# Linear attention and a leaky-ReLU feed-forward on one core: chunk order, transpose path and scheduler changed

## The chip, the cores and the metric

One core of a Trainium2 chip runs the whole kernel. The metric is the device time in microseconds of one execution; three runs of the kernel before gave 204.39 us as their median (204.13 to 206.44).

## What is computed

A recurrent attention with a decaying state runs over 4 batches, 8 heads, 768 positions and a head size of 48; its output, as 3072 tokens of 384 numbers, goes through a feed-forward of width 2048.

```python
for t in range(S):
    cur = einsum('bhd,bhe->bhde', u * k[t], v[t])
    y[t] = einsum('bhd,bhde->bhe', r[t], state + cur)
    state = w[t][..., None] * state + einsum('bhd,bhe->bhde', k[t], v[t])
x = y.transpose(0, 2, 1, 3).reshape(B * S, H * D)
h = x @ w_in                      # 384 -> 2048
out = maximum(0.01 * h, h) @ w_out  # 2048 -> 384
```

Inputs and output are float32; matmuls run in bfloat16.

## The kernel before

The positions are cut into chunks of 128, so there are 24 chunks, six for each batch. For each chunk the attention makes these steps, one instruction or one short group of instructions each:

- SP's DMA queue loads w, k, r and v (L290, 192 KB each, in pieces of 192 B) into one of 11 `in` buffers.
- ACT takes the logarithm of w (L310, `lw`); TensorE sums it from the chunk's far end with the triangular matrix `trev` (L325) and, where there is a state, gives its totals per head (L330). DVE adds `lw` to that sum (L340, `ci`); ACT takes the two exponents `er` (L347) and `ek` (L353), and DVE multiplies r and k by them (L360, L366) into the two halves of `rk`.
- TensorE transposes `rk` in eight pieces (L379) into the PSUM tile `sc`; DVE and ACT copy the halves out (L387, L389) as `rkT`. TensorE makes the scores from `rkT` (L450), into `sc` again, and DVE masks them into `m` (L471).
- GpSimd prepares the diagonal part (L406, L410, with DVE's L414, then L418 into `vs`), casts v (L316) and decays the state (L439, `sb`). TensorE's sums (L461) and DVE's addition (L485) make the next state.
- TensorE multiplies state and masked scores by their operands (L497, L501) into `yp`, DVE adds `vs` and makes `y` (L512). TensorE transposes `y` in three pieces (L521), and ACT copies it into the chunk's columns of `xT` (L527).

The feed-forward takes a block of chunks, here always one. Its up part is four groups of 12 matmuls of 128 columns (L553) into one of two `hp` tiles, each emptied by ACT with the leaky ReLU into `g` (L587). Its down part is four groups of 4 matmuls of 384 columns (L605) into one of two `op` tiles, which DVE copies out (L616) and SP's queue stores (L620). The weights come in 8 DMAs of 768 KB (L243, L248) and are cast by DVE and ACT in halves (L266, L268).

Chunks run through batch 0, then batch 1, and so on, so that a chunk's state is that of the chunk just before it. The order of the instructions on each engine isn't the order of the program. The class `Plan` keeps each step's engine, duration, dependencies and priority, plays the engines against each other, and puts the steps out by the times at which they started in that play. Attention has priority `P0 = n * 10`, the feed-forward 1000 and more, ACT's leaky ReLU 5. The logarithm of chunk n must not be planned before the first up group of chunk n - LEAD, and its loads not before the cumulation of chunk n - AHEAD. `Ring` gives buffers out in turn, as the program is written. On the chip each engine, and SP's queue, takes its instructions strictly in that order.

Of the kernel before, what the change touches and what calls it, by code (L numbers as in the profile page):

```python
# [14 lines left out]

class Plan:
# [3 lines left out]
    LAT = {"PE": 0.28, "DVE": 0.07, "ACT": 0.07, "POOL": 0.07, "SP": 0.07}  # L20

    def __init__(self):
        self.eng, self.dur, self.fn, self.deps, self.pri, self.wire = [], [], [], [], [], []

    def add(self, eng, dur, fn, deps, pri, wire=None):

        i = len(self.eng)
        self.eng.append(eng)
        self.dur.append(dur)
        self.fn.append(fn)  # L30
        self.deps.append(sorted({d for d in deps if d is not None}))
        self.pri.append(pri)
        self.wire.append(wire)
        return i

    def order(self):
        n = len(self.eng)
        users = [[] for _ in range(n)]
        left = [len(d) for d in self.deps]
        for i, d in enumerate(self.deps):  # L40
            for j in d:
                users[j].append(i)
        ready_at = [0.0] * n
        start, done = [None] * n, [0.0] * n
        free = {e: 0.0 for e in self.ENGINES}
        coming = {e: [] for e in self.ENGINES}
        ready = {e: [] for e in self.ENGINES}
        dma_free = 0.0
        for i in range(n):
            if not left[i]:  # L50
                heapq.heappush(coming[self.eng[i]], (0.0, i))
        events = [(0.0, e) for e in self.ENGINES]
        heapq.heapify(events)
        count = 0
        while events:
            now, e = heapq.heappop(events)
            if free[e] > now + 1e-9:
                continue
            while coming[e] and coming[e][0][0] <= now + 1e-9:
                _, i = heapq.heappop(coming[e])  # L60
                heapq.heappush(ready[e], (self.pri[i], i))
            if not ready[e]:
                if coming[e]:
                    heapq.heappush(events, (coming[e][0][0], e))
                continue
            _, i = heapq.heappop(ready[e])
            start[i] = now
            count += 1
            free[e] = now + self.dur[i]
            if self.wire[i] is None:  # L70
                done[i] = free[e] + self.LAT[e]
            else:
                dma_free = max(dma_free, free[e]) + self.wire[i]
                done[i] = dma_free + 1.5
            heapq.heappush(events, (free[e], e))
            for j in users[i]:
                left[j] -= 1
                ready_at[j] = max(ready_at[j], done[i])
                if not left[j]:
                    f = self.eng[j]  # L80
                    heapq.heappush(coming[f], (ready_at[j], j))
                    heapq.heappush(events, (max(ready_at[j], free[f]), f))
        assert count == n, (count, n)
        self.start, self.done = start, done
        return sorted(range(n), key=lambda i: (start[i], i))


class Ring:


    def __init__(self, tiles):
        self.tiles = tiles
        self.steps = [[] for _ in tiles]
        self.n = -1

    def take(self):
        self.n += 1
        k = self.n % len(self.tiles)
        old, self.steps[k] = self.steps[k], []
        return Use(self.tiles[k], old, self.steps[k])  # L100


class View:


    def __init__(self, use, t):
        self.t, self.old, self.steps = t, use.old, use.steps


class Use:  # L110
    def __init__(self, t, old, steps):
        self.t, self.old, self.steps = t, old, steps
# [3 lines left out]
def kernel(  # L116
# [23 lines left out]
    NPE = 24  # L140
    LEAD = 4
    AHEAD = 5

    WEIGHTS = [(2, 14)] * 4 + [(4, 34)] * 4
    blocks = [1] * NCH
# [3 lines left out]
    psum = ctx.enter_context(tc.tile_pool(name="psum", bufs=1, space=bass.MemoryType.PSUM))  # L149

    def ring(name, count, shape, dtype, where=None):
        return Ring([(where or pool).tile(shape, dtype, name=f"{name}{i}") for i in range(count)])


    trev = pool.tile([128, 128], BF16, name="trev")
    maskb = pool.tile([128, 128], BF16, name="maskb")
# [6 lines left out]

    in_r = ring("in", 11, [128, 1536], F32)
    lw_r = ring("lw", 3, [128, H, 64], BF16)
    ci_r = ring("ci", 2, [128, H, D], F32)
    er_r = ring("er", 3, [128, H, D], F32)
    ek_r = ring("ek", 2, [128, H, D], F32)
    rk_r = ring("rk", 4, [128, 2, H, 64], BF16)
    rkT_r = ring("rkT", 4, [128, 2 * NP, 128], BF16)  # L170
    vb_r = ring("vb", 6, [128, H, D], BF16)
    ru_r = ring("ru", 2, [128, H, D], F32)
    dg_r = ring("dg", 3, [128, H], F32)
    vs_r = ring("vs", 4, [128, H, D], F32)
    m_r = ring("m", 3, [128, 2, NP, 128], BF16)
    a_r = ring("a", 3, [128, NP, 2], F32)
    sx_r = ring("s", 3, [128, NP, 2, D], F32)
    sb_r = ring("sb", 3, [128, NP, 2, D], BF16)
    y_r = ring("y", 4, [128, H, D], BF16)
    g_r = ring("g", 4, [128, NJ, max(blocks) * L], BF16)  # L180
    o_r = ring("o", 4, [128, DM], F32)

    hp_r = ring("hp", 2, [128, 512], F32, psum)
    op_r = ring("op", 2, [128, DM], F32, psum)
    cp_r = ring("cp", 1, [128, 512], F32, psum)
    yp_r = pp_r = ring("yp", 1, [128, 512], F32, psum)
    sc_r = ring("sc", 1, [128, 2, NP, 128], F32, psum)

    with tc.manual_schedule():
        nc.scalar.preload_act_table_set("natural_log_exp_and_others")  # L190
        for t in lw_r.tiles + rk_r.tiles:
            nc.vector.memset(t[:], 0.0)
        for t in a_r.tiles:
            nc.gpsimd.memset(t[:], 0.0)
        nc.vector.memset(ones[:], 1.0)
        nc.vector.memset(trev[:], -1.0)

        nc.gpsimd.affine_select(
            out=trev[:], in_=trev[:], compare_op=ALU.is_ge, fill=0.0,
            base=0, pattern=[[-1, 128]], channel_multiplier=1,  # L200
# [7 lines left out]

# [7 lines left out]
        def step(eng, dur, fn, pri, reads=(), writes=(), deps=(), wire=None):  # L216

            d = list(deps)
            for x in writes:
                d += x.old  # L220
            i = plan.add(eng, dur, fn, d, pri, wire)
            for x in (*reads, *writes):
                x.steps.append(i)
            return i

        def dve(n, src=60):
            return (src + n) / 960.0 + 0.05

        def act(n, src=180):
            return (src + n) / 1200.0 + 0.02  # L230

# [4 lines left out]
        JQ = NJ // NQ  # L236

        def weight_steps(q, which, pri):
            st = in_r.take()

            def load(st=st, q=q):
# [11 lines left out]
            ld = step("SP", 0.45, load, pri, writes=[st], wire=2.2)  # L253
            made = []
            for half, eng in ((0, "DVE"), (1, "ACT")):
                def cast(st=st, q=q, half=half, eng=eng):
# [8 lines left out]
                    if eng == "DVE":  # L265
                        nc.vector.tensor_copy(out=o, in_=i)  # L266
                    else:
                        nc.scalar.copy(out=o, in_=i)  # L268
                d = 0.65 if eng == "DVE" else act(768, 224)
                made.append(step(eng, d, cast, pri, reads=[st], deps=[ld]))  # L270
            (win_s if which == 0 else wout_s).append(made)


        xt_steps, cums, lns = [], [], []
        prev = None
        for n in range(NCH):
            b, c = divmod(n, C)
            t0 = c * L
            P0 = n * 10
            for i, (before, pri) in enumerate(WEIGHTS):  # L280
                if n == before:
                    weight_steps(i % NQ, i // NQ, pri)
            first, last = c == 0, c == C - 1
            slot = in_r.take()
            wn, kn, rn, vn = (
                View(slot, slot.t[:, i * DM : (i + 1) * DM].rearrange("p (h d) -> p h d", h=H)) for i in range(4))
            lds = []
            for src, use in ((w, wn), (k, kn), (r, rn), (v, vn)):
                def load(src=src, use=use, b=b, t0=t0):
                    nc.sync.dma_start(  # L290
                        out=use.t, in_=src[b, :, t0 : t0 + L, :].rearrange("h p d -> p h d")
                    )
                lds.append(step(
                    "SP", 0.45, load, P0, writes=[slot], wire=0.97,
                    deps=[cums[n - AHEAD]] if n >= AHEAD else []))
            if n == 0:
                u_ld = step(
                    "SP", 0.5,
                    lambda: nc.sync.dma_start(
                        out=ub[:], in_=u.rearrange("h d -> (h d)").partition_broadcast(128)  # L300
                    ),
                    P0, wire=0.6,
# [3 lines left out]
            lw = lw_r.take()  # L306
# [234 lines left out]
        for nb, size in enumerate(blocks):  # L541
# [17 lines left out]
            for ch in chs:  # L559
                for q in range(4):  # L560
                    m2.append((ch, q, g, (ch - chs[0]) * L))
# [97 lines left out]
```

## Time and profile before

| what | value |
|---|---|
| median of three runs | 204.39 us |
| the profiled execution's span | 203.9 us |
| its first matmul starts at | 4.49 us |
| its last stretch of down matmuls | 196.75 to 200.02 us |
| TensorE busy | 179.8 us (88%) |
| DVE, ACT, GpSimd busy | 140.6, 120.7, 102.4 us |
| DMA | 30.46 MB, mean 149 GB/s |

The profile is of one execution. "Busy" counts a matmul from its start to its modelled end, and matmuls overlap in the pipeline, so a busy TensorE is not one at its peak. A row of the groups names line, engine and operation, the tiles written and read, shapes and count, then busy us and mean ns, and then the idle time before these instructions with what ended it. The slices cut the span into 40 equal parts of 5.1 us; a digit is the busy share in tenths.

### The profile page before, as it was taken

The page shows a single profiled execution, that of the slowest core. Times are in us where ns is not written, and L with a number is a line of the kernel's source. Part 1 is how long each engine was busy: PE and PEld are TensorE (multiplying, and loading weights), DVE is VectorE, ACT ScalarE, POOL GpSimd, SP SyncE. Part 2 cuts the span into 40 slices and gives each one's busy share as a digit, 9 for nine tenths or more (in the row PEclk, how much of TensorE's full clock was granted, in tenths as well). Part 3 has the DMA queues.
Part 4 walks back from the last instruction along what each step waited for, and adds up shares of the span by engine and source line. Part 5 has one row for each costly group of instructions (what it writes and reads, how often), then busy time and mean ns, then how long its engine had stood idle before and what let it go on. Part 6 is the DMA issues. An engine that isn't in the chain of part 4 may idle for free.

```text
span 203.9 us, 6000 instructions
## 1 busy us (share of the span) xinstructions
PE 179.8 (88%) x2448; PEld 141.5 (69%) x2448; DVE 140.6 (69%) x231; ACT 120.7 (59%) x265; POOL 102.4 (50%) x126
## 2 busy tenths in 40 slices
PE   0436866999999999699997999999999999999992
PEld 0326754677878878477785777878887787788770
DVE  6588379758889994999769987876885585431111
ACT  3334985667875568267674675766865756644430
POOL 2581094248879995988869967365321110100000
PEclk9999995799999999999999999999999999999999
DMA  6999999999999999999979874691101101110002
GB/s 126 201 292 364 171 230 378 249 196 177 201 184 218 181 191 222 196 189 199 217 155 240 163 166 107 119 189 46 39 2 43 39 3 42 39 39 23 27 33 77
DMA packets 107178, 30.46 MB, mean 149 GB/s; under 512 B 100368, under 2 KB 105616, under 8 KB 107152
## 3 DMA queue, kind: packets, MB, share of 16 engines
q1 hardware_dynamic: 107152, 30.09, 69.4%
q8 instruction: 19, 0.31, 0.7%
q14 instruction: 7, 0.06, 0.1%
HBM read 25.36 MB, written 4.72 MB: 148 GB/s over the span
## 4 chain that ended last, share of the span: by engine, by line
PE 68%; DVE 11%; ACT 6%; DMA 5%; POOL 3%; issue 2%; SPq 1%; DVEq 0%
PE op L605 26%; PE hp L553 25%; PE sc L379 5%; PE sc L450 3%; DVE rk L366 2%; DMA in<-in_r_dram 2%; DMA in<-in_w_dram 2%; PE yp L501 2%; DVE m L471 2%; PE cp L325 2%; DVE rkT L387 2%; DVE rk L360 2%; ACT g L587 2%; PE yp L461 1%; PE yp L521 1%
## 5 line engine op out<-in xcount | busy, mean ns | idle before, releaser
L587 ACT ACTIVATE g<-hp 128x512 bf16<-128x512 f32 x96 | 57.3, 599 | 48.1 <-PE hp L553 47.5
L553 PE MATMUL hp<-xT,w_in_b 128*128 128x128 bf16 x1152 | 80.4, 220 | 1.3 <-ACT xT L527 0.9
L605 PE MATMUL op<-w_out_b,g 128*128 128x384 bf16 x384 | 78.2, 330 | 0.0
L553 PEld LDWEIGHTS <-w_in_b 128*128 128x128 bf16 x1152 | 70.5, 99 | 9.0 <-issue 1.0
L605 PEld LDWEIGHTS <-g 128*128 128x128 bf16 x384 | 33.3, 98 | 14.2 <-issue 0.7
L471 DVE TENSOR_TENSOR m<-sc,maskb 128x1024 bf16<-128x1024 f32 x24 | 29.3, 1220 | 11.4 <-PE sc L450 9.9
L406 POOL TENSOR_TENSOR ru<-in,ub 128x384 f32<-128x384 f32 x24 | 24.9, 1037 | 16.5 <-DMA in<-in_r_dram 15.7
L439 POOL TENSOR_TENSOR sb<-s,a 128x384 bf16<-128x384 f32 x20 | 18.5, 924 | 25.3 <-ACT a L432 23.4
L418 POOL TENSOR_TENSOR vs<-in,dg 128x384 f32<-128x384 f32 x24 | 22.3, 931 | 17.1 <-DVE y L512 12.1
L616 DVE COPY o<-op 128x384 f32<-128x384 f32 x24 | 13.3, 552 | 19.3 <-PE op L605 19.2
L410 POOL TENSOR_TENSOR ru<-ru,in 128x384 f32<-128x384 f32 x24 | 25.7, 1071 | 0.4
L379 PE MATMUL sc<-ident,rk 128*128 128x128 bf16 x192 | 19.2, 230 | 5.6 <-DVE rk L360 3.2
L389 ACT COPY rkT<-sc 128x512 bf16<-128x512 bf16 x24 | 14.1, 586 | 14.5 <-PE sc L379 7.1
L366 DVE TENSOR_TENSOR rk<-in,ek 128x384 bf16<-128x384 f32 x24 | 21.8, 907 | 0.0
L360 DVE TENSOR_TENSOR rk<-in,er 128x384 bf16<-128x384 f32 x24 | 18.3, 765 | 3.4 <-ACT er L347 2.3
L379 PEld LDWEIGHTS <-rk 128*128 128x128 bf16 x192 | 13.4, 101 | 10.3 <-DVE rk L360 4.3
L316 POOL CAST vb<-in 128x384 bf16<-128x384 f32 x24 | 12.9, 536 | 10.5 <-DMA in<-in_v_dram 8.6
L414 DVE TENSOR_REDUCE dg<-ru 128x8 f32<-128x384 f32 x24 | 13.1, 545 | 6.4 <-POOL ru L410 6.3
L512 DVE TENSOR_TENSOR y<-yp,vs 128x384 bf16<-128x384 f32 x24 | 13.2, 552 | 5.3 <-PE yp L501 4.5
L340 DVE TENSOR_TENSOR ci<-cp,lw 128x384 f32<-128x384 f32 x24 | 13.2, 548 | 3.8 <-PE cp L330 2.9
L347 ACT ACTIVATE er<-cp 128x384 f32<-128x384 f32 x24 | 11.9, 495 | 6.2 <-DVE ci L340 6.1
L310 ACT ACTIVATE lw<-in 128x384 bf16<-128x384 f32 x24 | 12.6, 523 | 2.5 <-DMA in<-in_w_dram 2.4
(39 smaller groups left out, 160.8 us busy)
## 6 DMA issues: line engine op xcount, KB each, us to landing
in<-in_w_dram SPq DMA_DIRECT2D x24, 192.0 KB, 4.4
in<-in_k_dram SPq DMA_DIRECT2D x24, 192.0 KB, 4.6
in<-in_r_dram SPq DMA_DIRECT2D x24, 192.0 KB, 4.6
in<-in_v_dram SPq DMA_DIRECT2D x24, 192.0 KB, 4.3
out_dram<-o SPq DMA_DIRECT2D x24, 192.0 KB, 3.2
in<-in_moe_w_in_dram SPq DMA_DIRECT2D x4, 768.0 KB, 8.3
in<-in_moe_w_out_dram SPq DMA_DIRECT2D x4, 768.0 KB, 7.7
ub<-in_u_dram SPq DMA_DIRECT2D x1, 192.0 KB, 4.4
```

What stands on the lines that cost most here:

```text
L360: lambda rk=rk, rn=rn, er=er: nc.vector.tensor_tensor(out=rk.t[:, 0, :, 0:D], in0=rn.t, in1=er.t[:], op=ALU.mult),
L366: lambda rk=rk, kn=kn, ek=ek: nc.vector.tensor_tensor(out=rk.t[:, 1, :, 0:D], in0=kn.t, in1=ek.t[:], op=ALU.mult),
L379: nc.tensor.transpose(trv[:, a, g, :], rk.t[:, a, 2 * g : 2 * g + 2, :].rearrange("p h d -> p (h d)"), ident[:])
L389: nc.scalar.copy(out=o, in_=i)
L406: lambda ru=ru, rn=rn: nc.gpsimd.tensor_tensor(out=ru.t[:], in0=rn.t, in1=ubv, op=ALU.mult),
L410: lambda ru=ru, kn=kn: nc.gpsimd.tensor_tensor(out=ru.t[:], in0=ru.t[:], in1=kn.t, op=ALU.mult),
L418: lambda vs=vs, vn=vn, dg=dg: nc.gpsimd.tensor_tensor(out=vs.t[:], in0=vn.t, in1=dg.t[:].unsqueeze(2).to_broadcast([128, H, D]), op=ALU.mult),
L439: lambda sb=sb, s_in=s_in, a_in=a_in: nc.gpsimd.tensor_tensor(out=sb.t[:].rearrange("p g a d -> p (g a) d"), in0=s_in.t[:].rearrange("p g ...
L471: lambda m=m, sc=sc: nc.vector.tensor_tensor(out=m.t[:].rearrange("p a g t -> p (a g) t"), in0=sc.t[:].rearrange("p a g t -> p (a g) t"), ...
L553: nc.tensor.matmul(hp.t[:, a * N : (a + 1) * N], lhsT=w_in_b[:, t, (j + a) * 128 : (j + a + 1) * 128], rhs=xT[:, t, c0 : c0 + N], start=(a ...
L587: lambda hp=hp, g=g, j=j, J=J, N=N: nc.scalar.activation(out=g.t[:, j : j + J, 0:N], in_=hp.t[:, 0 : J * N].rearrange("p (a n) -> p a n", ...
L605: nc.tensor.matmul(op.t[:], lhsT=g.t[:, j, off : off + 128], rhs=w_out_b[:, j, :], start=(j == 0), stop=(j == NJ - 1))
```

## The change

- Chunk n is now chunk n // 4 of batch n % 4: the four batches take turns. The states are kept per batch (six `s` buffers for three, four `sb` for three), and the stores go to the rows that belong to the chunk.
- For the first four chunks (`BOTH_PE`), which have no state, TensorE makes a second sum with a new constant `tinc`, into an `op` tile, and ACT takes `ek` from it. DVE's addition `ci` falls away there.
- From the 13th chunk on (`RK_DMA`, `Y_DMA` = 12), `rk` and `y` are transposed by DMAs of SP's queue, from SBUF to SBUF. TensorE's eleven transposes, the two evictions and the copy into `xT` fall away for these chunks.
- The feed-forward's blocks are six of one chunk, seven of two and four of one. A block of two has up matmuls of 256 columns, in groups of six.
- `LEAD` goes from 4 to 5 and `AHEAD` from 5 to 6; `in` has 10 buffers, `g` 3 of double size, `o` 5, `ek` 3.
- w_in's loads come after the loads of chunk 3, w_out's after those of chunk 4. In the kernel before they came after chunks 1 and 3.
- `Plan` gives out buffers as it plays (`Buf`): a step starts once every buffer that it takes is free. A step can name two engines, and the first that is free takes it (evictions, casts, copies of `o` and `xT`). The play also counts what the DMA rings hold.

```diff
-    NPE = 24
-    LEAD = 4
-    AHEAD = 5
-    WEIGHTS = [(2, 14)] * 4 + [(4, 34)] * 4
-    blocks = [1] * NCH
+    RK_DMA = 12
+    Y_DMA = 12
+    BOTH_PE = 4
+    LEAD = 5
+    AHEAD = 6
+    blocks = [1] * 6 + [2] * 7 + [1] * 4
...
+    DMA_LATENCY = 1.5
+    RING = {0.97: 64, 2.15: 24, 0.55: 8, 0.6: 8, 1.75: 64, 0.65: 24}
...
+                    while flying and sum(x for _, x in flying) + size > 150:
+                        free[e] = max(free[e], flying.pop(0)[0])
+                    dma_free = max(dma_free, free[e] + 0.2) + wire
+                    flying.append((dma_free, size))
+                    self.done[i] = dma_free + self.DMA_LATENCY
...
+        wq = {4: [(0, 0), (1, 0), (2, 0), (3, 0)], 5: [(0, 1), (1, 1), (2, 1), (3, 1)]}
         for n in range(NCH):
-            b, c = divmod(n, C)
+            c, b = divmod(n, B)
+            for q, which in wq.get(n, []):
+                weight_steps(q, which, P0 - 8)
...
+            if n < BOTH_PE:
+                cq = Buf("op")
+                s_cq = step({"PE": 0.165},
+                    lambda e, cq=cq, lw=lw: nc.tensor.matmul(
+                        cpv(cq), lhsT=tinc[:], rhs=lw.t[:, :, 0:D], start=True, stop=True, ...),
+                    P0, deps=[s_ln], reads=[lw], takes=[cq])
+                s_ek = step({"ACT": 0.495},
+                    lambda e, cq=cq, ek=ek: nc.scalar.activation(out=ek.t[:], in_=cpv(cq), func=AF.Exp),
+                    P0, deps=[s_cq], reads=[cq], takes=[ek])
...
-            if n < NPE:
+            if n < RK_DMA:
...
+                    s_T.append(step({"DVE": 0.42, "ACT": 0.59}, evac, P0, deps=[s_tr], reads=[tr], takes=[rkT]))
             else:
                 s_T = [step(
+                    {"SP": 0.6},
+                    lambda e, rk=rk, rkT=rkT: nc.sync.dma_start_transpose(
                         out=rkT.t[:], in_=rk.t[:].rearrange("p a h d -> p (a h d)")),
+                    P0, deps=[s_r, s_k], reads=[rk], takes=[rkT], wire=1.75)]
...
-            if n < NPE:
+            if n < Y_DMA:
...
             else:
                 xt_steps.append(step(
+                    {"SP": 0.6},
+                    lambda e, y=y, col=col: nc.sync.dma_start_transpose(
                         out=xT[:, :, col : col + L], in_=y.t[:].rearrange("p h d -> p (h d)")),
+                    P0 + 1, deps=[s_ye], reads=[y], wire=0.65))
...
+                pri = 1000 + nb * 32 + j
+                s_up = step({"PE": J * KT * (N / 2400 + 0.0027)}, up, pri, takes=[hp],
+                    deps=[xt_steps[ch] for ch in chs] + win_s[j * 128 // 512])
...
+                    pri = 1000 + nb * 32 + 32 + (ch - chs[0]) * 8 + q + 0.5
...
+                s_o = step({"DVE": 0.55, "ACT": 0.5}, ocopy, 3, deps=[s_dn], reads=[op], takes=[o])
+                cc, bb = divmod(ch, B)
+                row = bb * S + cc * L
```

## The prediction

> **What bounds the kernel now.** I began with the page: the busy line of the engines and their slices.
>
> ```profile
> PE 179.8 (88%) x2448; PEld 141.5 (69%) x2448; DVE 140.6 (69%) x231; ACT 120.7 (59%) x265; POOL 102.4 (50%) x126
> PE   0436866999999999699997999999999999999992
> PEclk9999995799999999999999999999999999999999
> DMA  6999999999999999999979874691101101110002
> ```
>
> TensorE is the only engine near its limit, and it is full from slice 9 on; the first eight slices (some 41 us) are thin, and DMA is full in all of them. So the time has two parts with different limits: a start that waits for transfers, and a long stretch that is TensorE work. I cut them at 42 us, when the last w_out cast (L266, 39.5 us) is over.
>
> ```profile
> 0.00:42.00 42.00, 25.20 (x292) 18.92 (x293) 29.29 (x51) 23.15 (x45) 18.15 (x30) 0.92 0.99 249
> 42.00:200.03 158.03, 154.55 (x2158) 122.61 (x2156) 110.77 (x179) 97.54 (x220) 84.22 (x97) 1.00 0.64 125
> ```
>
> The columns are the stretch, its length, busy us and count of PE, PEld, DVE, ACT, POOL, then clock, DMA share and GB/s. Busy counts a matmul's pipeline too, so I priced matmuls by the time to the next one in dense stretches, from the chain of waits and, for the short ones, from consecutive starts in the trace.
>
> ```profile
> 18.47 1.46 PE hp L553 x12
> ...
> 190.15 0.65 PE op L605 x4
> 190.80 0.67 PE hp L553 x12
> ```
>
> An up matmul costs 55.8 ns (0.67/12), a down matmul 162 ns (0.65/4), a transpose 56 ns, a score 31, a state or sum matmul 42, an intra matmul 25, the cumulation 162 with 25 for each of its four totals. Times the counts of the groups (1152, 384, 192 + 72, 192, 160, 192, 24 and 80) that is 64.3 + 62.3 + 14.8 + 6.0 + 6.7 + 4.8 + 5.9 = 164.8 us of work. The span is then 4.5 (first matmul) + 164.8 + 30.7 of gaps + 3.9 (after the last matmul: copy and store) = 203.9. Before 42 us, 120 ups, 23 downs and 149 others are 16.6 us of work, so 20.9 of the 30.7 us of gaps lie there; 9.8 lie after, two of them named:
>
> ```profile
> PE yp L497 <- POOL ru L406: 1.4, 1, 1.4
> PE yp L497 <- DVE s L485: 1.3, 1, 1.3
> ```
>
> With what stands around them they are 3.0 us: the state product of a chunk waits for the chunk just before it, whose inputs came late. The other 6.8 us are crumbs below 0.4 us, of which 2.3 stand ahead of transposes (L379, L521).
>
> **The transposes (chunks 12 to 23).** Removed from TensorE: 12 x (8 + 3) x 56 ns = 7.4 us, and 12/20 of the 2.3 us of crumbs, 1.4 us.
>
> ```profile
> L379 PE MATMUL sc<-ident,rk 128*128 128x128 bf16 x192 | 19.2, 230 | 5.6 <-DVE rk L360 3.2 <-DVE rkT L387 1.5 <-DVE rk L366 0.4
> L389 ACT COPY rkT<-sc 128x512 bf16<-128x512 bf16 x24 | 14.1, 586 | 14.5 <-PE sc L379 7.1 <-DVE rkT L387 6.6 <-DVE dg L414 0.4
> L387 DVE COPY rkT<-sc 128x512 bf16<-128x512 bf16 x24 | 10.1, 419 | 4.4 <-PE sc L379 2.4 <-ACT rkT L389 1.8
> ```
>
> The evictions that go (12 x 0.59 and 12 x 0.48 on ACT, 12 x 0.42 on DVE) I count at nothing: after 42 us ACT is busy 62% and DVE 70% beside a full TensorE, and that is their cover. Added: two DMAs per chunk on SP's queue. The trace has no DMA transpose. The nearest rows:
>
> ```profile
> in<-in_w_dram SPq DMA_DIRECT2D x24, 192.0 KB, 4.4
> out_dram<-o SPq DMA_DIRECT2D x24, 192.0 KB, 3.2
> in<-in_moe_w_in_dram SPq DMA_DIRECT2D x4, 768.0 KB, 8.3
> ```
>
> A load of 1024 pieces of 192 B holds the queue 0.97 us (12 loads issued from 43.65 to 55.3 us, the queue full); rk is 1024 runs of 256 B. The plan in the diff allows 0.6 + 0.2 + 1.75 + 1.5 = 4.05 us from issue to use. Lower bound: the store row with a load's length, 3.2 + 0.42 = 3.6, early by 0.4. Upper bound: the weight row, 8.3, late by 4.25. TensorE takes its instructions in order: if rkT is late, the scores wait at the head of its queue and the next up and down groups wait behind them. I take the load row, to which it is nearest in pieces: 3.6 with a short queue, 4.6 behind one more load, so late by 0.55 in half of the chunks: 12 x 0.28 = 3.3 us (bounds: 0, since an early landing gives nothing back, and 51). The y transposes cost nothing: xT stands ready some 10 us ahead of its first up matmul today (chunk 23: 181.6 to 192.0, chunk 14: 118.9 to 131.7), and LEAD 5 adds a chunk. Behind them on SP's queue stand loads and stores. With the plan's 1.75 + 0.65 us a chunk puts 3.9 + 0.55 + 2.4 = 6.85 us on the queue, which is all that TensorE's chunk of 6.9 us leaves; but only some 7 of the 12 chunks still have loads to come, so 12 x 2.95 + 7 x 3.9 = 63 us stand against 83, and the 20 us over are the cover.
>
> The Trainium skill speaks against this step: "VectorE: DVE Perf Modes", section "The three transpose paths", lists 1309 ns for a 128x128 bf16 transpose by DMA against 390 by TensorE and advises TensorE where PSUM will do. Taken one after another, eleven would be an estimated 14.4 us a chunk and the queue would set the end, some 90 us later. "Advanced Engine Details and Errata", section "X-Bar Transpose (TRN2)", holds transposes to be as fast as plain DMAs, by which the step costs nothing. No row here shows either, and neither enters the sum.
>
> **The start.** Loads of chunks 0 to 3 now go ahead of w_in. Today w_in's first cast is at 14.87 us behind two chunks; two more are 8 x 0.97 = 7.8, so 22.7, and the others every 2.2 us to 29.4. Then chunk 4 (3.9) and w_out: casts at 35.4 to 42, some 2.5 us later than today. In that time four chunks without state lie ready instead of one chain. Work by 42 us: chunks 0 to 3, 8 x 56 + 8 x 31 + 4 x 42 + 8 x 25 + 3 x 56 + 2 x 162 ns = 1.56 each, 6.2; chunk 4, 1.7; ups of the three chunks that the three g buffers hold, 3 x 2.68 = 8.0; six groups of downs on the two op buffers, 3.9: in all 20, against 16.6 today. Bounds: 17, if w_out's lateness eats it, and 23, if all four groups of three chunks fit. TensorE's second product for the early exponents adds 4 x 162 ns = 0.65 us and takes the addition (L340, 0.55 us) out of four chunks' chains, which wait for loads anyway: no gain counted. The new constant's set-up (0.17 and 0.29 us by the rows of trev) stands behind trev's, under the first load.
>
> The clock: the twelve ups at 18.47 took 1.46 us against 0.67 later, and the granted clock read 0.5 from 31.2 to 38.0 us. A start with less to do on TensorE before 22 us could meet the same again; the bound is 12 groups at 1.3, 8 us, mostly under the wait for w_out. "TensorE: Matmul & The Clock Gate", Part 1, tells of a half clock until some 3.4 us of steady work; by that alone the loss would be an estimated 1.7 us. The row is larger, and it decides my upper bound.
>
> **Chunks round the batches; blocks; the plan.** The state that a chunk needs is now four chunks old, which takes away the 3.0 us. Blocks of two: 336 matmuls of 256 columns for 672 of 128; on the line through 128 (55.8) and 384 (162) one is 108.9 against 111.6: 0.9 us. Freely given buffers and engines: nothing counted, since the engines that they relieve are not the bound.
>
> **The sum.** Work 164.8 - 7.4 - 0.9 + 0.65 = 157.2. After 42 us: 157.2 - 20 = 137.2 of work, and gaps of 6.8 - 1.4 = 5.4, in proportion to the work (137/148) 5.0, + 3.3. Span 42 + 137.2 + 8.3 + 3.9 = 191.4. The profiled span is 0.5 us below the median of the runs, 204.39, so 191.9: **192.0 us**.
>
> **Rivals.** *Slower: rkT late on TensorE's queue.* If a transpose DMA lands like something halfway to the weight row, 2 us after the plan, each of 12 chunks stops TensorE that long: 24 us in place of 3.3, 212.6, say **213**. It decides from 18 us on, 1.5 us a chunk. For it: nothing but bounds is known of this DMA. Against it: blocks of matmuls that don't need rkT could stand ahead if the plan's time is right. *No change: the start gives nothing.* With the half clock through the ups and w_out late, work by 42 us is 15 and gaps after stay at 12: 42 + 142.2 + 12 + 3.9 + 0.5 = 200.6, **201**. For it: DMA is full in the first 42 us whatever the order. *More:* 23 by 42 us and no DMA waits: 42 + 134.2 + 5 + 3.9 + 0.5 = 185.6. That fewer transposes move than said is excluded by the counts in the diff.
>
> **Chances.** Forecast with its larger variant 0.75, no change 0.12, slower 0.13; 2% is about what a measurement of this kernel can tell from no change. The range runs from 184, below the larger variant, to 203, beyond the no-change case.
>
> **What would show it.** Transposes: sc with ident 96 and yp with ident 36 in place of 192 and 72; rkT's landing 3.6 to 4.6 us; no wait of TensorE for rkT above 0.6. Start: first up at 22 to 23 us, some 20 us of work by 42. The two waits for sb gone. Gaps after 42 us near 8. I am wrong if TensorE's waits name the DMA transposes, or if the stretch after 42 us is above 150 us.

## Result, and the profile after

| | before | after |
|---|---|---|
| median of four runs each, side by side | 205.03 us (204.13 to 206.44) | 196.84 us (196.46 to 197.09) |
| span of the profiled execution | 203.9 us | 194.9 us |

The ratio is 0.9593, with a 95% interval of 0.9535 to 0.9651: the changed kernel is 4% faster. The forecast was 192.0 us, with 184 to 203 as its range. The direction came true and the time lies in the range, 4.8 us above the forecast, about as far as from the 201 us of the rival in which the start gives nothing. The experiments show more than that: without the DMA transposes nothing is left of the gain, and they bring it only where the plan issues them in time, a thing to which the prediction gave no price.

The page of the changed kernel, its busy line and three of its slices rows:

```profile
PE 174.4 (89%) x1984; PEld 129.8 (67%) x1984; DVE 129.4 (66%) x206; ACT 114.5 (59%) x251; POOL 104.7 (54%) x127
...
PE   0557699899999999899899999899999999999992
...
PEclk9999999999999999999999999999999999999999
DMA  6999999997999999999996999997999953212012
```

TensorE has 464 matmuls fewer and is 5.4 us less busy; it is still the engine that is full. The dip of the granted clock in slices 7 and 8 of before is gone. DMA is now near full up to slice 32, where it was up to slice 22 in the kernel before: the chunks' loads are spread over a longer stretch, and the transposes have joined them.

The stretches of the changed kernel, with the same columns as before (stretch, length, busy us and count of PE, PEld, DVE, ACT, POOL, clock, DMA share, GB/s):

```profile
0.00:42.00 42.00, 28.32 (x333) 21.42 (x334) 28.01 (x51) 24.60 (x47) 20.65 (x32) 1.00 1.03 250
42.00:191.51 149.51, 146.11 (x1653) 108.33 (x1651) 100.81 (x155) 89.88 (x204) 84.02 (x95) 1.00 0.87 161
191.51:194.94 3.43, 0.00 (x0) 0.00 (x0) 0.56 (x1) 0.00 (x0) 0.00 (x0) 1.00 0.16 57
```

The long stretch is 149.5 us for 158.0 us: 8.5 of the 9.0 us by which the span is shorter lie there, the rest in the tail. With the prices per matmul that the prediction used, counted over the trace, the 194.9 us read as follows (before by the same count in brackets): work by 42 us 18.0 (16.6); work after 42 us 139.0 (148.0); gaps after 42 us 10.2 (9.7); tail 3.4 (3.9). So the gain of 9.0 us is 9.0 us of work that TensorE no longer has after 42 us, of which 1.4 us has moved ahead of it and 7.6 us is gone for good. Gaps did not shrink at all: they are 0.5 us longer, which the shorter tail gives back. The prices are those at full clock, so in this count what a half clock adds stands among the gaps.

Two lines of the chain of waits (start, length, instructions):

```profile
25.64 1.46 PE hp L592 x12
...
188.26 3.26 PE op L619 x20
```

The twelve first ups take 1.46 us, exactly as in the kernel before and twice as long as later ones, although the clock row shows full speed there. From one to the next it is 107 ns, for 56 later, up to 29.5 us. In the kernel with all transposes on TensorE (below) the same twelve take 1.46 us too, and there the clock's record does show half speed, from 25.4 to 28.8 us. The last downs cost 163 ns each (3.26/20), so the price list holds for the changed kernel too.

The groups of TensorE's transposes, the issues of the DMA transposes (median us from issue to landing), and what TensorE waited for (us in total, times, longest):

```profile
L414 PE MATMUL sc<-ident,rk 128*128 128x128 bf16 x96 | 10.6, 248 | 5.1 <-ACT rkT L423 2.0 <-DVE rk L401 1.5 <-DVE rk L396 1.0
...
L557 PE MATMUL yp<-ident,y 128*128 128x128 bf16 x36 | 4.5, 242 | 0.1
```

```profile
rkT<-rk SPq DMA_TRANSPOSE x12, 4.0
xT<-y SPq DMA_TRANSPOSE x12, 3.1
```

```profile
PEld L482 <- DMA rkT<-rk: 1.8, 4, 1.0
...
PE sc L482 <- DMA rkT<-rk: 0.7, 1, 0.7
PE yp L493 <- DVE rk L401: 0.7, 1, 0.7
```

Half of the transposes are left, 96 and 36. The DMA that takes the place of the others lands after 4.0 us, and TensorE stands for it at five places, at most 2.5 us together (0.7 at a matmul, 1.8 at weight loads, a single one up to 1.0). The two waits of 1.4 and 1.3 us for a state are not in the list any more.

SP's queue is where the DMAs are issued. A piece of its timeline in the changed kernel (start, time that the instruction holds the queue, line, transfer); `rk` of chunk 12 was written at 89.6 us, that of chunk 13 at 94.4:

```profile
89.27 0.92 SPq L321 DMA_DIRECT2D in<-in_v_dram  x1
90.29 1.66 SPq L430 DMA_TRANSPOSE rkT<-rk  x1
92.05 0.52 SPq L638 DMA_DIRECT2D out_dram<-o  x1
92.62 0.42 SPq L321 DMA_DIRECT2D in<-in_w_dram  x1
93.14 0.64 SPq L321 DMA_DIRECT2D in<-in_k_dram  x1
94.45 1.29 SPq L430 DMA_TRANSPOSE rkT<-rk  x1
```

These two stand in the queue almost where their `rk` becomes ready: 0.65 us and 0.06 us after. Over the twelve chunks the issue comes 1.4 us after `rk` on the mean (3.3 at most), the landing 4.0 us after that, and the scores 0.9 us later still, 6.3 us in all. These rows turn out to be the ones that matter.

### The profile page after: what moved, and what is told of

The parts are those of the page before. It is cut to its first block, busy times and chain, and to the rows that moved or that the text cites. A ratio compares the mean times of both kernels' runs of the same rounds, so it can differ in the third digit from the quotient of the medians.

```text
span 194.9 us, 5056 instructions
## 1 busy us (share of the span) xinstructions
PE 174.4 (89%) x1984; PEld 129.8 (67%) x1984; DVE 129.4 (66%) x206; ACT 114.5 (59%) x251; POOL 104.7 (54%) x127
## 4 chain that ended last, share of the span: by engine, by line
PE 60%; DVE 13%; POOL 8%; DMA 7%; issue 6%; ACT 5%; SPq 0%; DVEq 0%; POOLq 0%; ACTq 0%
PE op L619 25%; PE hp L592 22%; PE sc L482 3%; DMA in<-in_w_dram 3%; PE sc L414 3%; DMA rkT<-rk 2%; POOL ru L438 2%; DVE m L503 2%; POOL vs L450 2%; POOL ru L442 2%; PE yp L537 2%; PE cp L352 2%; DVE rk L401 2%; DVE rk L396 1%; DVE dg L446 1%
## 5 line engine op out<-in xcount | busy, mean ns | idle before, releaser
L592 PE MATMUL hp<-xT,w_in_b 128*128 128x128 bf16 (+1 forms) x816 | 78.5, 244 | 1.4 <-ACT g L607 1.2
L619 PE MATMUL op<-w_out_b,g 128*128 128x384 bf16 x384 | 76.2, 326 | 0.0
L592 PEld LDWEIGHTS <-w_in_b 128*128 128x128 bf16 x816 | 61.8, 99 | 11.7 <-issue 1.6
L438 POOL TENSOR_TENSOR ru<-in,ub 128x384 f32<-128x384 f32 x24 | 25.0, 1040 | 19.2 <-DMA in<-in_r_dram 18.2
L396 DVE TENSOR_TENSOR rk<-in,er 128x384 bf16<-128x384 f32 x24 | 20.4, 848 | 4.8 <-ACT er L368 4.0
L630 DVE COPY o<-op 128x384 f32<-128x384 f32 x10 | 5.6, 558 | 23.4 <-PE op L619 13.1
L346 POOL CAST vb<-in 128x384 bf16<-128x384 f32 x24 | 16.0, 667 | 4.2 <-DMA in<-in_v_dram 4.2
L548 DVE TENSOR_TENSOR y<-yp,vs 128x384 bf16<-128x384 f32 x24 | 13.2, 549 | 4.6 <-PE yp L537 4.6
L414 PE MATMUL sc<-ident,rk 128*128 128x128 bf16 x96 | 10.6, 248 | 5.1 <-ACT rkT L423 2.0
L385 DVE TENSOR_TENSOR ci<-cp,lw 128x384 f32<-128x384 f32 x20 | 11.0, 548 | 4.0 <-PE cp L357 3.6
L462 ACT ACTIVATE a<-cp 64x4 f32<-64x4 f32 x40 | 6.7, 168 | 10.9 <-DVE ci L385 6.1
L352 PE MATMUL cp<-lw,trev 128*128 128x384 bf16 x24 | 8.5, 356 | 4.8 <-ACT lw L340 4.8
## 6 DMA issues: line engine op xcount, KB each, us to landing
in<-in_w_dram SPq DMA_DIRECT2D x24, 192.0 KB, 4.4
in<-in_k_dram SPq DMA_DIRECT2D x24, 192.0 KB, 3.9
in<-in_r_dram SPq DMA_DIRECT2D x24, 192.0 KB, 4.2
in<-in_v_dram SPq DMA_DIRECT2D x24, 192.0 KB, 4.1
out_dram<-o SPq DMA_DIRECT2D x24, 192.0 KB, 3.2
ub<-in_u_dram SPq DMA_DIRECT2D x1, 192.0 KB, 4.7
```

The costliest lines, as they stand in the source:

```text
L346: lambda e, vb=vb, part=part: nc.gpsimd.tensor_copy(out=vb.t[:], in_=part(3)),
L396: lambda e, rk=rk, er=er, part=part: nc.vector.tensor_tensor(out=rk.t[:, 0, :, 0:D], in0=part(2), in1=er.t[:], op=ALU.mult),
L414: nc.tensor.transpose(trv(tr)[:, a, g, :], rk.t[:, a, 2 * g : 2 * g + 2, :].rearrange("p h d -> p (h d)"), ident[:])
L438: lambda e, ru=ru, part=part: nc.gpsimd.tensor_tensor(out=ru.t[:], in0=part(2), in1=ubv, op=ALU.mult),
L592: nc.tensor.matmul(hp.t[:, a * N : (a + 1) * N], lhsT=w_in_b[:, t, (j + a) * 128 : (j + a + 1) * 128], rhs=xT[:, t, c0 : c0 + N], start=(a ...
L619: nc.tensor.matmul(op.t[:], lhsT=g.t[:, j, off : off + 128], rhs=w_out_b[:, j, :], start=(j == 0), stop=(j == NJ - 1))
```

## The experiments

All ratios below are to the kernel before, run on the same chip, with their 95% interval. "Work" and "gaps" are counted as above; both come from one profiled execution. Where two experiments are compared, the uncertainty given is that of the difference of their ratios (root of the sum of the squared half intervals) times 205 us.

The theories carry letters in the expectations. W: the work that leaves TensorE is the gain. P: the rest of the change is, its plan and its order. S: the slack from the longer lead is what hides the DMAs. D: the DMA queue becomes a second bound when more goes through it. Q, formed after the first results: it is the place of the transpose among the loads on an in-order queue.

### Which part holds the gain

**All transposes back on TensorE**, the rest of the change kept:

```diff
-    RK_DMA = 12
-    Y_DMA = 12
+    RK_DMA = 24
+    Y_DMA = 24
```

> The changed kernel with all transposes back on TensorE (chunks 12 to 23 too), the plan made anew. Theory W (work): the gain is the work that left TensorE, 12 x 11 x 56 ns = 7.4 us; so the time rises by 7 to 9 us, to 204 to 206 us, as good as the kernel before. Rival P (plan and order): the gain comes from the order of the chunks and from the plan, and the DMA transposes give back in waits what they take off; then the time stays within 2 us of the changed kernel, 195 to 199.

Measured: 206.77 us, ratio 1.0015 [0.9983, 1.0047]. Nothing is left of the gain. The rest of the change without the DMA transposes brings none, so P falls, and on top of that rest the transposes are worth 4.2%, 8.7 us (± 1.4). The ledger says where the rest went: 164.4 us of work, of which 18.2 us by 42 us, 1.6 us more than in the kernel before; but 13.0 us of gaps after 42 us against 9.7. What the start brings is lost again after it. The group of the transposes shows one place:

```profile
L414 PE MATMUL sc<-ident,rk 128*128 128x128 bf16 x192 | 18.9, 230 | 6.9 <-DVE rk L401 2.3 <-DVE rk L396 2.0 <-ACT rkT L423 1.3
```

The idle time ahead of the 192 transposes is 6.9 us; the same 192 had 5.6 us in the kernel before, which is 1.3 of the 3.3 us of longer gaps. Why this order of instructions leaves more gaps was not separated.

**One kind of transpose alone.** `y` by DMA with `rk` on TensorE, and the other way round:

```diff
-    RK_DMA = 12
+    RK_DMA = 24
```

> The changed kernel with only the y transposes of chunks 12 to 23 by DMA; the rk transposes go back to TensorE. Theory W (work, hidden by slack): work rises by 12 x 8 x 56 ns = 5.4 us against the changed kernel, so about 0.985 of the kernel before, 202 us. Rival: the y path alone costs as much as it takes off, since its landing delays the up matmuls; then 1.00, no better than with all transposes on TensorE.

```diff
-    Y_DMA = 12
+    Y_DMA = 24
```

> The changed kernel with only the rk transposes by DMA from the 13th chunk; y is transposed by TensorE in all chunks. By work, 2.0 us more than the changed kernel: 0.969 of the kernel before. From the run with y alone by DMA, which came out at 0.998 against 1.0015 with none, y is worth 0.0035, so 0.963. If the DMA queue is the second bound, twelve transposes fewer on it give the 2.0 us back: 0.955 to 0.96.

Measured: `y` alone 204.10 us, ratio 0.998 [0.9941, 1.0018]; `rk` alone 198.62 us, ratio 0.9602 [0.9542, 0.9662]. For `y` alone W's 0.985 was missed, and the rival's 1.00 holds; for `rk` alone the 0.969 that work gives lies outside the interval. With `rk` alone the kernel is as fast as with both (0.9593), and `y` alone is worth 0.7 us (± 1.0) against all on TensorE. The 36 transposes of `y` are 2.0 us of work, but little or none of it comes back as time: with `rk` alone the work is 159.0 us for 157.0, and the gaps after 42 us are 8.9 us for 10.2. `rk` gives more than its work: 96 transposes are 5.4 us, and the step from all on TensorE to `rk` alone is 8.5 us (± 1.4). The rest fits with the gaps after 42 us, which fall from 13.0 to 8.9 us: without the transposes and the two evictions, the one `sc` tile is taken once for each of these chunks and not twice. No run shows that this is the reason.

### The order of the chunks and of the weights

**Batch after batch again**, the rest kept:

```diff
-            c, b = divmod(n, B)
+            b, c = divmod(n, C)
...
-                cc, bb = divmod(ch, B)
+                bb, cc = divmod(ch, C)
```

> The changed kernel with batch after batch in place of turns; all else as changed. Theory W: the order of the chunks is worth no more than the two waits for the state (3.0 us) and the start (1.5 us): 197 to 201 us. Rival P: the order is what pays, 203 us and more.

Measured: 198.04 us, ratio 0.9596 [0.9525, 0.9667], against 0.9593 with the chunks going round. The order of the chunks is worth 0.1 us (± 1.9), so not the 3.0 us that were counted. The profiled execution has 12.2 us of gaps after 42 us, 4.6 us of them ahead of state and sum matmuls (2.3 us when the chunks go round), yet no wait of over 0.2 us for a state: the two big waits of before do not come back with the old order. So it was not the order of the chunks that took them away; which other part of the change did, was not separated.

**The weights sooner.** In the first kernel both weights go back to where they were before, after chunks 1 and 3; in the second, w_out comes right behind w_in:

```diff
-        wq = {4: [(0, 0), (1, 0), (2, 0), (3, 0)], 5: [(0, 1), (1, 1), (2, 1), (3, 1)]}
+        wq = {2: [(0, 0), (1, 0), (2, 0), (3, 0)], 4: [(0, 1), (1, 1), (2, 1), (3, 1)]}
```

> The changed kernel with the weights' loads where the kernel before had them (w_in after chunk 1, w_out after chunk 3). If the late weights ate the gain of the start, w_out's last cast comes near 39 us in place of 45.3, TensorE's work by 42 us goes from 18.0 us to about 21, and the time falls to 193 to 195 us. Rival: the start is bound by all that must be loaded, and chunks that come later cost what weights that come sooner bring: 196 to 198 us.

```diff
-        wq = {4: [(0, 0), (1, 0), (2, 0), (3, 0)], 5: [(0, 1), (1, 1), (2, 1), (3, 1)]}
+        wq = {4: [(0, 0), (1, 0), (2, 0), (3, 0)]}
+        wq[4] += [(0, 1), (1, 1), (2, 1), (3, 1)]
```

> The changed kernel with w_out's loads straight after w_in's, ahead of chunk 4's loads (3.9 us sooner). If the start is limited by w_out (last cast at 45.3 us), the down matmuls start near 35.5 us in place of 39.5, TensorE does 20 us of work by 42 us in place of 18.0, and the time falls by 1 to 2 us, 0.95 to 0.955 of the kernel before. Rival: chunks 4 to 7, whose inputs come 8.6 us after chunk 4's turn for all of w_out, are what the up matmuls wait for next, and the time stays, 0.957 to 0.97.

Measured: weights as before 201.34 us, ratio 0.9748 [0.9701, 0.9795], slower than both expectations; w_out sooner 199.59 us, ratio 0.9645 [0.958, 0.971], as its rival had it. The stretches of the first:

```profile
0.00:42.00 42.00, 25.51 (x274) 19.06 (x275) 24.47 (x46) 22.93 (x41) 15.76 (x27) 0.92 0.98 246
```

and of the second:

```profile
0.00:42.00 42.00, 29.12 (x322) 21.32 (x323) 25.74 (x47) 24.93 (x45) 15.96 (x27) 1.00 1.03 250
42.00:84.00 42.00, 39.42 (x522) 29.57 (x517) 37.33 (x57) 30.46 (x75) 36.83 (x41) 1.00 1.07 196
```

With the weights early, the half clock of the kernel before is back (0.92 over the stretch; the records show half speed from 31.0 to 37.8 us), the work by 42 us is 16.5 us, as before, and the time is 3.2 us (± 1.5) above the changed kernel's. So the late weights are worth something, as the prediction had it, though less work than it said. With w_out sooner the work by 42 us is 19.9 us, the 20 of the prediction; but the inputs of chunk 4 and those behind it now come later, and the gaps from 42 to 84 us are 6.3 us for 4.7. No gain is left of it. The likely reading is that a microsecond pushed into the first 42 us by one transfer is taken back when the transfer that it displaced is due; this was not followed transfer by transfer.

### Where the DMA transposes pay, and where not

**The kernel before with the same DMA transposes.** It has a switch for them; nothing else of the change is in it:

```diff
-    NPE = 24
+    NPE = 12
```

> The kernel before with one thing changed: the transposes of its chunks 12 to 23 go by DMA (its own old plan, batch after batch, weights as before). Theory W: 205.0 - 7.4 = 197.6, so 196 to 200 us, nearly all of the gain with a fraction of the change. Rival P: batch after batch, the later rkT stops TensorE in every chunk, 203 to 207 us.

Measured: 205.30 us, ratio 0.9928 [0.9893, 0.9963]. This missed what W expected by far. The work is 157.3 us, as low as in the changed kernel, and only 1.5 us of time is gained. The gaps took the rest: 22.2 us by 42 us (21.0 before) and 16.3 us after (9.7), of which 7.2 us lie from 84 to 126 us, where the first DMA transposes are; a half clock from 121.5 to 128.3 us adds to them. That stretch, and two of TensorE's waits from 42 us on:

```profile
84.00:126.00 42.00, 38.27 (x511) 30.20 (x510) 33.89 (x51) 21.76 (x52) 32.13 (x39) 0.95 1.11 195
```

```profile
PE hp L553 <- DMA xT<-y: 2.4, 2, 1.2
PE sc L450 <- DMA rkT<-rk: 2.0, 3, 1.1
```

TensorE waits for both kinds of transposes, for `y`'s too, which the prediction had counted at nothing because `xT` stood ready 10 us ahead. The time is the one that the rival gave. That work leaves TensorE is needed, then, and is not enough.

**More slack for it**, and less slack for the changed kernel. If S were right, the first would gain and the second lose:

```diff
-    NPE = 24
-    LEAD = 4
-    AHEAD = 5
+    NPE = 12
+    LEAD = 5
+    AHEAD = 6
```

> The kernel before with DMA transposes from the 13th chunk and with LEAD 5 and AHEAD 6 of the change; its old plan otherwise. Theory S: the slack is what was lacking, 0.965 to 0.975 of the kernel before (198 to 200 us), against 0.993 with LEAD 4. Rival Q: the old plan puts the waits in the wrong places whatever the distance, 0.985 to 1.00.

```diff
-    LEAD = 5
-    AHEAD = 6
+    LEAD = 4
+    AHEAD = 5
```

> The changed kernel with LEAD 4 and AHEAD 5, the values of the kernel before. Theory S (slack): DMA transposes pay only if attention runs far enough ahead of the feed-forward to hide their 4 us; with one chunk less the waits of TensorE for rkT and xT come back and half of the gain is lost, 0.975 to 0.99 of the kernel before (200 to 203 us). Rival Q (the plan's picture of the DMA queue is what matters, not the distance): within 1% of the changed kernel, 0.955 to 0.97.

Measured: more slack 212.25 us, ratio 1.0376 [1.0319, 1.0433]; less slack 196.86 us, ratio 0.965 [0.9616, 0.9684]. S falls on both sides: less slack costs 1.2 us (± 1.4), and more slack is slower than either expectation. Its 212.25 us are near the 213 of the prediction's "slower" rival, but not by that rival's cause. SP's timeline of this kernel, in which `rk` of chunk 12 was written at 95.6 us and that of chunk 13 at 101.2:

```profile
95.16 0.88 SPq L290 DMA_DIRECT2D in<-in_w_dram  x1
...
99.18 0.93 SPq L620 DMA_DIRECT2D out_dram<-o  x1
...
101.55 2.45 SPq L290 DMA_DIRECT2D in<-in_r_dram  x1
104.09 0.60 SPq L290 DMA_DIRECT2D in<-in_v_dram  x1
104.78 0.65 SPq L620 DMA_DIRECT2D out_dram<-o  x1
105.53 0.38 SPq L290 DMA_DIRECT2D in<-in_w_dram  x1
106.01 0.72 SPq L290 DMA_DIRECT2D in<-in_k_dram  x1
106.78 1.24 SPq L290 DMA_DIRECT2D in<-in_r_dram  x1
108.12 1.62 SPq L397 DMA_TRANSPOSE rkT<-rk  x1
```

The transpose of chunk 12 is issued 12.5 us after its operand is there. Ahead of it in the queue stand most of three chunks' loads and two stores; and one load holds the queue for 2.45 us where the others here take 0.4 to 1.2. The landing itself takes no longer than elsewhere (median 3.3 us). Chunks 12 to 16 are issued 10.3 to 13.2 us late, and TensorE pays for it (waits of the stretch from 42 us on, and two stretches):

```profile
PE sc L450 <- DMA rkT<-rk: 5.0, 2, 2.8
```

```profile
84.00:126.00 42.00, 34.09 (x433) 25.11 (x431) 31.96 (x52) 19.38 (x47) 32.44 (x37) 0.93 1.10 196
126.00:168.00 42.00, 37.69 (x514) 29.98 (x515) 27.01 (x40) 21.39 (x48) 15.75 (x19) 0.86 0.63 126
```

From 84 to 126 us TensorE is busy 34.1 of 42 us (40.6 in the changed kernel), with 13.0 us of gaps that begin there, and the clock is at 0.93 and then 0.86: the half clock is back from 113.5 to 116.9 and from 123.7 to 137.4 us. By an estimate that is up to 8.5 us, half of these 17.1 us, so a large part of the loss may be the clock; what brings the clock down was not tested.

**The plan told less of the queue.** The new play counts the descriptors in the DMA rings and holds SP's queue when they exceed 150. With 600 it lets four times as many in; the kernel keeps every other part of the change:

```diff
-                    while flying and sum(x for _, x in flying) + size > 150:
+                    while flying and sum(x for _, x in flying) + size > 600:
```

> The changed kernel, planned as if the DMA rings held 600 descriptors an engine in place of 150, so that the plan lets some nine loads be in flight in place of two; nothing else is changed, and the chip's rings stay as they are. Theory Q (what matters is where the transposes stand on SP's queue, behind loads that block it): rk transposes are issued 4 us and more after rk is ready in place of 1.4, and the time rises to 0.975 to 1.00 of the kernel before. Rival: the limit in the plan is a detail, within 1% of the changed kernel, 0.955 to 0.97.

Measured: 205.61 us, ratio 0.9943 [0.9908, 0.9979]. One number in the planner is worth 7.2 us (± 1.4), nearly the whole gain. SP's timeline of this kernel (`rk` of chunk 12 written at 89.5 us) and its stretch, with that of the changed kernel below it:

```profile
94.01 0.98 SPq L321 DMA_DIRECT2D in<-in_w_dram  x1
95.10 0.93 SPq L321 DMA_DIRECT2D in<-in_k_dram  x1
96.13 2.15 SPq L430 DMA_TRANSPOSE rkT<-rk  x1
```

```profile
84.00:126.00 42.00, 36.68 (x386) 25.43 (x384) 34.28 (x51) 18.29 (x43) 32.93 (x38) 0.96 1.11 196
```

```profile
84.00:126.00 42.00, 40.55 (x441) 29.63 (x440) 34.94 (x55) 26.66 (x62) 28.31 (x33) 1.00 1.08 181
```

The transpose comes 6.6 us after its operand, and chunks 12 to 17 are issued 6.3 to 9.0 us late; 9.2 us of gaps lie from 84 to 126 us, 3.4 in the changed kernel. A plan that lets more loads be in flight puts more of them ahead of the transpose. The two traces show this apart from the rest: `rk` of chunks 12 to 16 is ready within 2 us of the same times in both kernels, and the scores made from it start 5.5 to 9.7 us later here. That is what Q says. TensorE's waits from 42 us on are then for `rkT` itself and, more, for the masked scores `m`, which come out of the late scores:

```profile
PE yp L537 <- DVE m L503: 2.2, 2, 1.2
PE sc L482 <- DMA rkT<-rk: 1.1, 1, 1.1
```

A part of the 7.2 us is the clock: the record shows half speed from 122.9 to 129.7 us, an estimated 3.4 us at most, half of that stretch. The one number makes the whole plan anew, and no run has it with all transposes on TensorE; that it acts through the transposes alone is therefore not shown.

**The transposes on a queue of their own.** The kernel before, once more with DMA transposes, issued now from ScalarE's queue, with the issue counted in the plan as ACT's time:

```diff
-    NPE = 24
+    NPE = 12
...
-                    "SP", 0.6,
-                    lambda rk=rk, rkT=rkT: nc.sync.dma_start_transpose(
+                    "ACT", 1.3,
+                    lambda rk=rk, rkT=rkT: nc.scalar.dma_start_transpose(
...
-                    "SP", 0.6,
-                    lambda y=y, col=col: nc.sync.dma_start_transpose(
+                    "ACT", 0.8,
+                    lambda y=y, col=col: nc.scalar.dma_start_transpose(
```

> The kernel before with its transposes from the 13th chunk by DMA, issued from ScalarE's queue in place of SP's (the old plan, LEAD 4). Theory Q: past the loads they are issued at once (0.1 us after rk is ready against 2.5 on average on SP's queue), and the 7.4 us of TensorE work come out as time: 0.965 to 0.975 of the kernel before. Rival: each issue holds ScalarE for 1.2 to 1.3 us and, waiting for DVE, the leaky ReLU behind it, so TensorE waits for hp: 0.99 to 1.02.

Measured: 202.75 us, ratio 0.9781 [0.9701, 0.9862], between the two expectations, and 3.0 us (± 1.8) better than the same on SP's queue. Two lines, from its issues and from SP's waits:

```profile
rkT<-rk ACTq DMA_TRANSPOSE x12, 4.6
```

```profile
SPq L620 <- DVE o L616: 57.7, 14, 8.4
```

The issue now follows `rk` after 0.14 us, for 2.5 us on SP's queue without the change (where chunks 12 to 15 took 3.5 to 6.7). The landing takes longer, though, so that from `rk` to the scores it is 6.7 us on the mean for 7.5. Of SP's 57.7 us of waits for a tile to store, 55.9 lie after 126 us; they say nothing of how full its queue was before. So another queue brings 3.0 of the 6.9 us by which the changed kernel beats the kernel before with DMA transposes on SP's queue. The rest stands in the ledger as 15.4 us of work by 42 us for 18.0, and as gaps after 42 us of 13.7 us for 10.2; how these divide among weights, clock and plan stays open.

**More of the same.** Transposes by DMA from the 9th chunk on:

```diff
-    RK_DMA = 12
-    Y_DMA = 12
+    RK_DMA = 8
+    Y_DMA = 8
```

> The changed kernel with the DMA transposes from the 9th chunk on. Theory W: four more chunks take 4 x 11 x 56 ns = 2.5 us off TensorE, 0.947 to 0.952 of the kernel before (194 to 195 us). Rival D (the DMA queue is the second bound: in the changed kernel it is full up to 156 us, and inputs land just as they are needed): the 2.4 us a chunk more on the queue delay the inputs, no gain or a loss, 0.96 to 0.98.

Measured: 198.81 us, ratio 0.973 [0.9692, 0.9767], 2.8 us (± 1.4) slower than from the 13th chunk, with 2.5 us less work. Its last stretch:

```profile
126.00:168.00 42.00, 38.46 (x383) 27.66 (x380) 26.61 (x38) 24.27 (x54) 24.84 (x28) 0.96 1.03 188
```

DMA is full there (share 1.03, in the changed kernel 0.86), TensorE is busy 38.5 us for 41.5, and its gaps are 7.95 us for 2.1. This fits D, and half speed from 144.3 to 147.7 us adds to it: with more transposes in it, a full DMA queue brings the last chunks' inputs late. That chain was not followed transfer by transfer.

None of the versions tried is faster than the changed kernel. Blocks of one chunk and early exponents by DVE were not run.

## Why the prediction was right, and which terms were not

**The direction held, and so did the core of the mechanism.** That transposes leave TensorE, and that TensorE's work sets the long stretch, was the largest single term (5.5 of 12.4 us), and without it nothing of the gain is left. The work came out at 157.0 us for 157.2. The landing of the DMA transposes, which no row of before showed, was put at 3.6 to 4.6 us by a load's row; the median is 4.0 and the single ones range from 3.1 to 5.1. TensorE's wait for `rkT`, 3.3 us in the sum, is 2.5 at most. One of its own signs of being wrong did come, though: TensorE's waits name the DMA transposes, and not all stay below 0.6 us. On the two rules of the Trainium skill that were set aside: eight pieces of 128x128 that land in 4.0 us are 0.5 us a piece, and the loads beside them land in 3.9 to 4.4 us. That agrees with "Advanced Engine Details and Errata", section "X-Bar Transpose (TRN2)", and not with the 1309 ns of "VectorE: DVE Perf Modes", section "The three transpose paths", if that price of one piece is taken for each of eight, one after another.

**The miss of 4.8 us**, term by term. Work by 42 us 18.0 for 20: 2.0. Gaps after 42 us 10.2 for 8.3: 1.9. Less work 0.2 and a shorter tail 0.5 the other way, and 0.3 for the last matmul's own length, which the sum left out: 3.5 us of span. The distance from span to time was 1.7 us for the 0.5 read from before: 1.2. That 0.5 set the span of one execution against the median of others; wherever a run has both numbers, its time is at least 1.7 us above its span. The rest of the miss is rounding and the median above the profiled run.

- *The start* failed in its transfers. The first up came at 25.6 us for 22 to 23, and w_out's casts began between 39.5 and 45.3 us for 35.4 to 42: pricing eight more loads at 0.97 us of queue time each was too little, probably since these transfers share full DMA engines (DMA share 1.03 by 42 us). The clock's record shows no half clock there any more, but the ups up to 29.5 us still run at half rate.
- *Chunks round the batches*, 3.0 us, is worth nothing that could be measured. The step took a wait's releaser for its cause: the waits for the state were gone, and stayed gone with the old order.
- *The transposes* were mis-sized the other way: 7.4 + 1.4 - 3.3 = 5.5 us were counted; on top of the rest 8.7 us were measured, and 8.5 us with `rk` alone. The 2.0 us of `y` were counted and did not come.
- *The cover on SP's queue*, "20 us over", was reckoned as capacity. With twelve chunks capacity did not decide: the same transposes on the same queue give 0.9928 or 1.0376 with only the lead, and the order that the plan makes from it, between them, and 0.9943 or 0.9593 with only the plan's limit.
- *The plan's count of the DMA rings* had no term at all, and this is the largest error. Freely given buffers and engines were put at nothing, since the engines that they relieve are not the bound; the count of the rings, in the same part of the diff, was passed over. Its limit is worth 7.2 us: with 600 for 150 the whole change brings some 1 us.

That the sum came as near as it did is in good part luck. It gave the rest of the change (start 3.4, order 3.0, blocks 0.9, less 0.65 for the second product, and crumbs) about 7 us and the transposes 5.5, as if each were worth the same without the other. They are not. The rest alone brings nothing (1.0015), and the transposes on top of it 8.7 us; the transposes alone bring 1.5 us (0.9928), and the rest on top of them 6.9. Which part "has" the gain depends on which is put in first, and a sum of separate terms can't say that. Blocks of two and the early exponents, 0.9 and 0.65 us, stay untested by themselves.

**The rivals.** The slower one named the right danger, a late `rkT` at the head of TensorE's queue, and with the wrong cause: not a slow landing (the medians are 3.3 to 4.6 us in all runs) but a late issue. It was held off by the plan. "No change" did not come about, though the work by 42 us fell short, 18.0 us for 20 and for the 15 of this rival, and the time is as near to its 201 us as to the forecast.

## What to carry to other kernels

Price a moved step not by its own row alone but by its place in the queue that takes it: here an in-order queue full of loads made a transfer of 4 us one of 10 to 18 from operand to landing, and the same twelve transfers kept TensorE waiting for 2.5 us at most where the order put them behind few loads. Where a planner writes the order, a change of its model of a resource is a change of the kernel, and belongs in the sum with the step that depends on it. Take each of two such parts away in turn, and not only one, before saying which of them pays. And a wait that vanishes from the list is no gain until one edit alone has brought it back.

## What the runs showed of the hardware

- A DMA transpose of 128x1024 bf16 holds the queue that issues it for 1.2 us at least (median 1.3 in the changed kernel) and up to 3.4 us (the kernel before with DMA transposes). It lands in 3.0 to 6.3 us from SP's queue; from ScalarE's, beside full loads on SP's, in 3.1 to 6.0 us, median 4.6.
- Issuing takes queue time: after 42 us a load of 192 KB holds SP's queue for 0.4 to 2.5 us, in the changed kernel and in the kernel before with DMA transposes and more slack alike, and up to 5.3 us in the first 42 us; all that stands behind waits. In the latter kernel the transpose of chunk 12 was issued 12.5 us after its operand was there.
- The granted clock's record can miss a half clock at the start: the first twelve ups took 1.46 us for 0.67 in a slice whose digit is 9, the rate that they had in the kernel whose record shows half speed there.
- The half clock comes back in the middle of a run, without a long pause. With the limit of 600 it holds from 122.9 us on, after 3.4 us in which TensorE was busy for 1.05 us and never idle for more than 1.2 us at a time; in the kernel with more slack it holds for 17.1 us between 113.5 and 137.4 us, in and behind a stretch with 13.0 us of gaps.
